# A recorded schedule gets a model of the DMA queue; transposes move between TensorE and DMA; outputs get a second PSUM bank

## The chip, the core and the metric

The kernel runs on one core of one Trainium2 chip. The metric is the device time of one execution in microseconds (us), as the median of several. PE is TensorE, PEld its weight loads, DVE is VectorE, ACT ScalarE, POOL GpSimd, SP SyncE, which issues all DMAs here. A transfer lands when its data can be used. PSUM is the memory that PE writes its results to; it is divided into banks.

## The reference, cut to what matters

```python
# q, k, v, f_logit: (4, 8, 768, 48) float32
f = 1.0 / (1.0 + np.exp(-f_logit))
for t in range(S):
    state = f[:, :, t, :, None] * state + np.einsum('bhd,bhe->bhde', k[:, :, t], v[:, :, t])
    y[:, :, t] = np.einsum('bhd,bhde->bhe', q[:, :, t], state)
x = y.transpose(0, 2, 1, 3).reshape(3072, 384)
out = np.maximum(x @ w_in, 0.0) ** 2 @ w_out      # w_in 384 x 2048, w_out 2048 x 384
```

It is a gated linear attention with a state per head, and a feed-forward with squared relu on its result.

## The kernel before

It works in 24 chunks of 128 tokens, six for each of four sequences. A chunk passes through a line of short steps on all engines: logarithms and sums of the gates (a1, p1), their exponentials (a2), scaled q and k (v1q, v1k, in the tile az), their transposes (p2 and v2 on PE and DVE or ACT, or t2 by DMA), scores (p3, v3), the result yp (p4), its bf16 copy ys (a3), the transpose of that (p6, v6, to xT), and the state sz for the next chunk (p5, s1, s2). The feed-forward's first layer (hp, L439) takes chunks 6 and later in threes, 384 columns wide; the second (op, L484) gives 128 tokens at a time.

No order is written down. Each step is given to a planner with its engines, durations, predecessors and buffers. The planner plays the program through, always starting the best ready step, and then records the instructions in that order. Each engine runs its own list in order. A planner that is wrong about time therefore makes engines stand behind an instruction whose data are late, while others could run.

```python
        plan.add(f"{n}{i}", "SP", 1.03, fn, take=["io_" + n], rank=0, land=1.9)      # a load: 1.03 us on SP, lands 1.9 us later
...
        plan.add(f"w{kind}{s}", "SP", 2.3, fn, take=["wst"], rank=0, land=1.9)       # a fourth of w_in or w_out
...
        xbar = i >= XBAR                                                             # XBAR = 8
        if xbar:
            plan.add(f"v2.{i}", "SP", 1.5, t2, after=[f"v1k.{i}", f"v1q.{i}"], take=["ts"], rank=-2, land=3.5)
        else:
            both(f"v2.{i}", 0.65, 1.0, v2, after=[f"p2.{i}"], take=["ts"], give=[f"tr:p2.{i}"])
...
        plan.add(f"s2.{i}", "POOL", 1.0, s2, after=[f"s1.{i}"] + ([f"p4.{i - 1}"] if c else []), give=[f"en:a2n.{i}"])
...
            tag = "h" if g == NG - 1 and tt else "o"                                 # the bank of an output; "o" is one bank
```

Loads go first in, first out: three chunks, w_in, three chunks, w_out, the rest. Dummy matmuls (idle, L513) fill PE's gaps until 40 us.

## Time and profile before

| | before |
|---|---|
| median time | 199.9 us (198.7 to 200.1) |
| span of the profile | 197.0 us |
| PE, DVE, ACT, POOL busy | 90%, 68%, 67%, 20% |
| bytes moved by DMA, share of the queue's time | 34.1 MB, 87.9% |
| DMA transposes | 16, of q and k of chunks 8 to 23 |

The prediction shows the lines that matter. One more view belongs here, the timeline of POOL in the kernel before, as it dates the arrival of the chunks. Columns: start, length, engine, line, operation, operands, and in brackets the idle time ahead with its releaser.

```profile
58.95 0.51 POOL L284 CAST vz<-io_v 128x384 bf16<-128x384 f32 x1 [0.76 <-DMA io_v<-in_v_dram]
...
62.81 0.51 POOL L284 CAST vz<-io_v 128x384 bf16<-128x384 f32 x1 [0.59 <-DMA io_v<-in_v_dram]
```

These are the casts of v for chunks 7 and 8; both start when the load lands.

### The profile page before, as it was taken

How to read it: one execution, taken by the hardware profiler on the slowest of the kernel's cores; microseconds unless marked ns; L12 is line 12 of the kernel's file. 1: busy time of each engine (PE TensorE's matmuls, PEld its weight loads, DVE VectorE, ACT ScalarE, POOL GpSimd, SP SyncE). 2: the span in 40 equal slices, each digit the busy share in tenths (PEclk: the TensorE clock that was granted, in tenths of full speed). 3: DMA queues.
4: the chain of work that ended last, by engine and by line, in shares of the span. 5: the costliest groups of instructions: out<-in, count | busy, mean ns of one | idle time of the engine just before them, and what ended most of it. 6: DMA issues, size and time to landing. Idle time of an engine off the chain costs nothing.

```text
span 197.0 us, 4806 instructions
## 1 busy us (share of the span) xinstructions
PE 178.3 (90%) x1837; PEld 120.4 (61%) x1837; DVE 134.0 (68%) x285; ACT 132.8 (67%) x281; POOL 38.5 (20%) x80
## 2 busy tenths in 40 slices
PE   5986888769899889998899999799999999999993
PEld 5865777668676556555566666466665666665661
DVE  4578878877779638887897897687889743343300
ACT  4362777757885436888898798686866958655410
POOL 5153001610133304202312320132331300000000
PEclk9999999999999999999999999999999999999999
DMA  7999999899889999999899999998999531111012
GB/s 129 188 163 295 367 167 203 196 379 240 172 164 227 171 223 215 206 193 190 169 200 212 208 207 163 213 195 183 203 215 190 113 95 40 42 39 37 31 58 80
DMA packets 123927, 34.39 MB, mean 175 GB/s; under 512 B 117248, under 2 KB 122368, under 8 KB 123904
## 3 DMA queue, kind: packets, MB, share of 16 engines
q1 hardware_dynamic: 123904, 34.09, 87.9%
q8 instruction: 14, 0.23, 0.5%
q14 instruction: 9, 0.07, 0.1%
HBM read 25.17 MB, written 4.72 MB: 152 GB/s over the span
## 4 chain that ended last, share of the span: by engine, by line
PE 47%; SPq 22%; DMA 20%; ACT 3%; DVE 2%; issue 2%; POOL 2%; POOLq 0%; ACTq 0%
PE op L484 22%; SPq L206 19%; PE hp L439 17%; DMA io_v<-in_v_dram 16%; DMA io_f<-in_f_logit_dram 4%; SPq L222 2%; PE yp L369 2%; PE at L346 2%; POOL vz L284 2%; PE ds L400 1%; DVE am L353 1%; PE xp L383 1%; PE pc L290 1%; SPq L333 1%; ACT ob L494 1%
## 5 line engine op out<-in xcount | busy, mean ns | idle before, releaser
L439 PE MATMUL hp<-xT,w_in 128*128 128x384 bf16 (+2 forms) x528 | 79.1, 282 | 3.7 <-ACT hr L446 2.4
L484 PE MATMUL op<-w_out,hT 128*128 128x384 bf16 x384 | 77.0, 326 | 1.6 <-ACT w_out L237 0.9
L439 PEld LDWEIGHTS <-w_in 128*128 128x128 bf16 x528 | 41.9, 97 | 20.2 <-issue 2.8
L446 ACT ACTIVATE hr<-hp 128x384 bf16<-128x384 f32 (+1 forms) x85 | 42.8, 509 | 15.1 <-PE hp L439 14.3
L484 PEld LDWEIGHTS <-hT 128*128 128x128 bf16 x384 | 35.4, 98 | 23.2 <-issue 2.1
L455 DVE TENSOR_TENSOR hT<-hr 128x384 bf16<-128x384 bf16 (+1 forms) x80 | 30.7, 390 | 23.0 <-ACT hr L446 22.0
L353 DVE TENSOR_TENSOR am<-at,ut 128x512 bf16<-128x512 f32 x48 | 31.4, 683 | 3.8 <-PE at L346 3.6
L417 POOL TENSOR_TENSOR sz<-tm,en 48x192 bf16<-48x192 f32 x40 | 21.1, 528 | 41.9 <-DVE tm L408 9.5
L284 POOL CAST vz<-io_v 128x384 bf16<-128x384 f32 x24 | 13.9, 581 | 72.8 <-DMA io_v<-in_v_dram 72.7
L453 ACT ACTIVATE hT<-hr 128x384 bf16<-128x384 bf16 (+1 forms) x40 | 21.5, 539 | 4.4 <-DVE hr L448 3.5
L279 ACT ACTIVATE e<-io_f 128x384 f32<-128x384 f32 x24 | 12.5, 521 | 15.0 <-DMA io_f<-in_f_logit_dram 14.8
L448 DVE TENSOR_SCALAR hr<-hp 128x384 bf16<-128x384 f32 (+1 forms) x35 | 20.1, 580 | 2.4 <-PE hp L439 2.1
L310 DVE TENSOR_TENSOR az<-io_k,ep 128x384 bf16<-128x384 f32 x24 | 14.0, 583 | 6.8 <-ACT ep L300 5.8
L314 DVE TENSOR_TENSOR az<-io_q,en 128x384 bf16<-128x384 f32 x24 | 13.8, 573 | 4.2 <-DMA io_q<-in_q_dram 4.2
L300 ACT ACTIVATE ep<-pc 128x384 f32<-128x384 f32 x24 | 11.8, 490 | 4.6 <-PE pc L293 4.5
L513 PE MATMUL idle<-zero 128*128 128x128 bf16 x141 | 13.4, 250 | 1.0 <-DVE zero L249 1.0
L494 ACT COPY ob<-op 128x384 f32<-128x384 f32 x18 | 8.5, 473 | 8.5 <-PE op L484 8.4
L280 ACT ACTIVATE pz<-e 128x384 bf16<-128x384 f32 x24 | 12.5, 523 | 0.8
L306 ACT ACTIVATE en<-pc 128x388 f32<-128x388 f32 (+1 forms) x24 | 11.9, 496 | 0.0
L513 PEld LDWEIGHTS <-zero 128*128 128x128 bf16 x141 | 10.6, 114 | 1.2 <-DVE zero L249 1.0
L290 PE MATMUL pc<-pz,ut 128*128 128x384 bf16 x24 | 8.0, 332 | 3.4 <-ACT pz L280 3.2
L377 ACT CAST ys<-yp 128x384 bf16<-128x384 f32 x15 | 7.2, 477 | 5.3 <-PE yp L369 5.1
(43 smaller groups left out, 146.4 us busy)
## 6 DMA issues: line engine op xcount, KB each, us to landing
io_f<-in_f_logit_dram SPq DMA_DIRECT2D x24, 192.0 KB, 4.2
io_k<-in_k_dram SPq DMA_DIRECT2D x24, 192.0 KB, 4.4
io_q<-in_q_dram SPq DMA_DIRECT2D x24, 192.0 KB, 4.4
io_v<-in_v_dram SPq DMA_DIRECT2D x24, 192.0 KB, 4.0
out_dram<-ob SPq DMA_DIRECT2D x24, 192.0 KB, 2.2
wi_f<-in_moe_w_in_dram SPq DMA_DIRECT2D x4, 768.0 KB, 7.4
wo_f<-in_moe_w_out_dram SPq DMA_DIRECT2D x4, 768.0 KB, 8.0
ts<-az SPq DMA_TRANSPOSE x16, 3.6
```

What stands on the lines that cost most here:

```text
L206: nc.sync.dma_start(t, srcs[n][b].rearrange("h s d -> s h d")[c * C:(c + 1) * C])
L284: nc.gpsimd.tensor_copy(vz[i % 3], st["v", i])
L310: nc.vector.tensor_mul(az[i % 3][:, H:, :D], st["k", i], st["ep", i])
L353: nc.vector.tensor_mul(t, st["at", i][x], ut4)
L417: nc.gpsimd.tensor_mul(nx[r, :, D * x:D * (x + 1)], st["tm", i][r, :, D * x:D * (x + 1)], st["en", i][r, HD:HD + NP].unsqueeze(2).to_broad ...
L439: nc.tensor.matmul(hp[:, x, :], w_in[:, ks, (f + x) * C:(f + x + 1) * C], xT[:, ks, lo:lo + W], start=(ks == 0), stop=(ks == KS - 1), skip ...
L446: nc.scalar.activation(hr[:, :m, :], st["hp", c0, f][:, :m, :], AFT.Relu)
L448: nc.vector.tensor_scalar_max(hr[:, :m, :], st["hp", c0, f][:, :m, :], 0.0)
L453: nc.scalar.activation(st["hT", g][:, f:f + m, lo:lo + W], hr[:, :m, :], AFT.Square)
L455: nc.vector.tensor_mul(st["hT", g][:, f:f + m, lo:lo + W], hr[:, :m, :], hr[:, :m, :])
L484: nc.tensor.matmul(st["o", i], hT[:, fs, tt * C:(tt + 1) * C], w_out[:, fs, :], start=(fs == 0), stop=(fs == FS - 1))
L513: nc.tensor.matmul(idle, zero, zero)
```

## The change

The intent is a planner with a model of how transfers queue. In this model SP is busy for a short time for each DMA, the transfers run one after the other, a ring of limited size makes SP wait, and data land 1.2 us after their last byte. Durations are fitted anew. With that model, the DMA transposes of q and k start at chunk 14 in place of 8; from chunk 18 the result is transposed by DMA too; four buffers in place of three for az, vz and en and three in place of two for ys; outputs of chunks 19 and 21 take the transposes' PSUM bank (23 already has another).

```diff
+    FIRST, RECEIPT = 0.4, 1.2
+    RING = 3000
...
+                    if s.data:
+                        us, size = s.data
+                        while sum(z for e, z in queue if e > end) + size > self.RING:
+                            end = min(e for e, z in queue if e > end)
+                        moved_to = max(moved_to, end + self.FIRST) + us
+                        queue.append((moved_to, size))
...
-                    fin = end + s.land
+                    fin = moved_to + self.RECEIPT if s.data else end + s.land
...
-    XBAR = 8
+    XBAR = 14
+    XBAR2 = 18
...
-                pz=2, az=3, vz=3, ts=3, am=2, ys=2, ep=2, en=3)
+                pz=2, az=4, vz=4, ts=3, am=2, ys=3, ep=2, en=4)
...
-            plan.add(f"{n}{i}", "SP", 1.03, fn, take=["io_" + n], rank=0, land=1.9)
+            plan.add(f"{n}{i}", "SP", 0.45, fn, take=["io_" + n], rank=0, data=(1.07, 1024))
...
-        plan.add(f"p1.{i}", "PE", 0.27, p1, after=[f"a1.{i}"] + ([f"p4.{i - 2}"] if i > 1 else []), ...
+        plan.add(f"p1.{i}", "PE", 0.26, p1, after=[f"a1.{i}"] + ([f"p4.{i - 3}"] if i > 2 else []), ...
...
-            plan.add(f"v2.{i}", "SP", 1.5, t2, after=[f"v1k.{i}", f"v1q.{i}"], take=["ts"], rank=-2, land=3.5)
+            plan.add(f"v2.{i}", "SP", 1.25, t2, after=[f"v1k.{i}", f"v1q.{i}"], take=["ts"], rank=-2, data=(1.7, 1024))
...
+        if xbar2:
+            plan.add(f"v6.{i}", "SP", 0.7, t6, after=[f"a3.{i}"] + ([f"v6.{i - 1}"] if o else []),
+                     take=["xT"] if o == 0 else [], give=[f"ys:a3.{i}"], rank=-2, data=(0.9, 384))
...
-            tag = "h" if g == NG - 1 and tt else "o"
+            tag = "h" if g == NG - 1 and tt else "tr" if i > max(XBAR, XBAR2) and i % 2 else "o"
```

Cut are the new durations of some twenty steps, most of them a few per cent shorter, and the fourth buffers' index arithmetic. The diff moves code, so line numbers shift: L439 (first layer) is now L459, L484 (second layer) L504, L237 (cast of weights on ACT) L248, L284 (cast of v) L295.

## The prediction

> **What bounds the kernel now.** I read the page first, its busy line and the slices.
>
> ```profile
> PE 178.3 (90%) x1837; PEld 120.4 (61%) x1837; DVE 134.0 (68%) x285; ACT 132.8 (67%) x281; POOL 38.5 (20%) x80
> ...
> PE   5986888769899889998899999799999999999993
> ...
> DMA  7999999899889999999899999998999531111012
> ```
>
> Two limits stand in a row. The DMA row is full until slice 31 (about 155 us) and then empty, while PE is at eight or nine tenths from slice 10 nearly to the end. Whether DMA or PE sets the end is told by the busy times in stretches of 15 us.
>
> ```profile
> 30.00:45.00 15.00, 11.59 (x189) 9.78 (x188) 12.28 (x25) 9.92 (x21) 4.32 (x8) 1.00 1.02 265
> 45.00:60.00 15.00, 13.63 (x185) 10.53 (x185) 11.27 (x26) 11.46 (x26) 2.65 (x4) 1.00 0.87 185
> ...
> 105.00:120.00 15.00, 15.00 (x143) 9.28 (x141) 12.71 (x27) 12.69 (x29) 3.53 (x7) 1.00 1.25 207
> ...
> 165.00:180.00 15.00, 15.00 (x97) 9.10 (x95) 5.38 (x15) 9.20 (x20) 0.00 (x0) 1.00 0.11 41
> ```
>
> Columns after the length: PE, PEld, DVE, ACT and POOL busy, then clock and DMA share. From 105 us PE has no slack, and it still works for 38 us after the last load has landed. So the end is PE work plus the idle time that PE collected before. Where that lies is told by the timeline of PE (in brackets the idle time ahead, and its releaser); I show its gaps between 39 and 76 us that matter, and the ends of that stretch.
>
> ```profile
> 39.03 1.50 PE L439 MATMUL hp<-xT,w_in 128*128 128x128 bf16 x24 [0.35 <-ACT xT L390]
> ...
> 42.87 0.83 PE L439 MATMUL hp<-xT,w_in 128*128 128x128 bf16 x12 [1.52 <-ACT hr L446]
> ...
> 50.24 0.81 PE L484 MATMUL op<-w_out,hT 128*128 128x384 bf16 x4 [0.94 <-ACT w_out L237]
> ...
> 65.80 0.33 PE L383 MATMUL xp<-ident,ys 128*128 128x128 bf16 x3
> ...
> 68.89 0.33 PE L400 MATMUL ds<-vz,az 128*128 128x96 bf16 x4 [0.88 <-POOL vz L284]
> ...
> 72.83 0.65 PE L484 MATMUL op<-w_out,hT 128*128 128x384 bf16 x3 [0.57 <-ACT ob L494]
> ...
> 74.92 0.33 PE L383 MATMUL xp<-ident,ys 128*128 128x128 bf16 x3
> ...
> 76.01 0.65 PE L439 MATMUL hp<-xT,w_in 128*128 128x384 bf16 x3
> ```
>
> With one of 0.33 us at 59.51 the gaps from 39.03 to 76.01 make 4.2 us. After 76 us the same view has five, 2.9 us in all, of which 1.95 wait for the cast of v on POOL (0.60, 1.00, 0.35). The 1.52 us goes back to ACT, which stands in line behind a cast whose weights have not landed:
>
> ```profile
> 41.81 0.51 ACT L237 CAST w_out<-wo_f 128x384 bf16<-128x384 f32 x1 [2.83 <-DMA wo_f<-in_moe_w_out_dram]
> ```
>
> The last two lines of PE above are the other half. At 76.01 the first 384-wide matmul of the feed-forward starts, the one for chunks 6 to 8 together. It waits for chunk 8. POOL casts v of chunk 7 at 58.95 us and PE transposes its result at 65.80, 6.9 us later. v of chunk 8, the first whose q and k go through the DMA transpose, is cast at 62.81, and its result is transposed at 74.92, 12.1 us later. By then 92 of the 96 output matmuls that chunks 0 to 5 give are done: PE is living on its last work.
>
> **What the Trainium skill says.** "TensorE: Matmul & The Clock Gate", section "Wait — 56ns, not 53.3ns?": start to start is N ÷ 2.4 GHz plus about 2.5 ns; 162.5 ns for 384 columns. The trace agrees: the chain has 12 output matmuls in 1.95 us. I use this form as unit price. The same page, "Architectural detail: the array is 16× 32×32, not 1× 128×128", says that ACT and DVE are strictly first in, first out; the 2.83 us above is such a case. "DMA: Bandwidth & Descriptors", section "Latency and other measured facts": about 600 ns to the first byte; the new model takes 0.4 us, and 1.2 us for the receipt. No trace splits it so, but the sum fits: the model (12 loads of 1.07, four weights of 2.75, 12 loads, one weight, plus 0.4 and 1.2, plus 0.45 for the first issue and 0.74 before it) puts the first w_out slice at 42.2 us, and the trace has its casts at 41.81. The old model (1.03, 2.3, 1.9) gives 38.9 with the same start, 2.9 us too early: just the length of that wait. "PSUM — Partial Sum Buffer", "Summary: rules for kernel authors": read one bank while matmuls write another; the 0.57 us on ob is the wait that a second output bank removes.
>
> **The change part by part.** (a) The model. It moves instructions and removes none. The order of PE's instructions, before and after, is known from the built programs; with unit prices I sum the real work (fillers left out) ahead of a landmark. Landmark one is the first matmul of chunk 3's feed-forward: 16.3 us of work in both. Landmark two is the first output matmul that needs the last w_out slice: 24.6 us before, 28.1 us after. That is the gain of the better model: 3.5 us of work that stood behind a wait now stands ahead of it. In the old kernel landmark two is at 50.24 us, and the loads ahead of it are unchanged, so it cannot come earlier.
>
> (b) Transposes of q and k for chunks 8 to 13 go back to PE: 6 × 8 = 48 matmuls at 55.5 ns, +2.7 us of PE, and six copies of about 0.6 us on DVE. Transposes of the result from chunk 18 leave PE: 6 × 3 at 55.5 ns, -1.0 us, and six copies of 0.3 us. Net on PE +1.7 us (159.0 to 160.6), all on the path. DMA loses six transposes; a chunk comes every 6.2 us with them (v of chunk 10 cast at 75.59, of chunk 23 at 155.91) and every 5.0 without (chunks 6 to 9), so about 7 us of DMA, which is beside PE's work and worth nothing by itself. Its real worth is that chunk 8 takes about 7 us instead of 12, so its columns are ready near 62.8 + 6.9 + 0.4 = 70.1 us.
>
> (c) Fourth buffers and the second output bank: at most the 0.57 us and part of the 2.9.
>
> The sum. Between 39.03 and 76.01 PE did 30.6 us of work by unit prices (16.3 to 46.9) in 37.0 - 4.2 = 32.7 us without gaps: factor 1.07. After the change: chunk 3 ready at about 38.0, as its transposes no longer stand behind the sums of chunk 4 (an estimate of mine); landmark two at 38.0 + 1.07 × 11.8 = 50.6, which just meets the weights; from there to the first 384-wide matmul 47.1 - 28.1 = 19.0, times 1.07 = 20.3, with 1.0 us of gaps (1.8 there before): 71.9 us, and chunk 8 is there at 70.1. That is 4.1 us earlier than 76.01. After it the old kernel did 112.1 us of work in 117.8 - 2.9 = 114.9 (factor 1.025); the new one has 160.6 - 47.1 = 113.5, times 1.025 = 116.3, with gaps of 2.0 (no waits for v, but DVE has more to copy at 75 to 90 us, where it was busy 13.37 of 15): PE ends at 190.2 instead of 193.8. The end behind it (copy, store: 3.2 us) stays. Span 193.4 instead of 197.0; time 199.9 - 3.6 = 196.3 us.
>
> **The rivals.** First, the transposes taken off the DMA pull the end in by their 7 us, to about 193, as the DMA row is full. Against: PE is full from 105 us on and has 38 us of work after the last load; loads that end near 148 shorten no PE work. Second, DVE and ACT become the bound: six copies more, at a stage where both have over 12 of 15 us busy; PE then loses 2 to 3 us more around 75 to 100 us, and the time stays at 199. For it: the copies all stand on DVE in the new order. Against: 15 relus move from DVE to ACT, and the sum of both engines changes by some 2 us in 267. Third, a new wait: the last chunk's result goes through the DMA, 3.6 us in the old trace for the larger transposes. Between the last attention matmul and the first use of its result stand 3 first-layer and 22 output matmuls, 25 × 162.5 ns = 4.1 us; if copy, issue and transfer take 6 us together, PE waits 2 us and the time is 198. For the short latency speaks that the DMA is nearly empty by then.
>
> **Range and chances.** The floor is no idle time after landmark two: 50.2 + 20.3 + 116.3 + 3.2 = 190.0 span, 192.9. The ceiling is the added 1.7 us with nothing gained but the chunk 8 wait, about 199. I take 193.3 to 199.0. Two per cent is 195.9, just under my figure: faster 0.43, same 0.52, slower 0.05.
>
> **What would show it.** Right: the first 384-wide matmul at 71 to 73 us; no wait of ACT or DVE over 1 us for the weights after 40 us; the last v cast near 148 us or before; PE busy 15.0 of 15 after 75 us; the last PE instruction near 190. Wrong: that matmul still at 75 or later (model step), new gaps of PE with DVE or ACT as releasers over 4 us in all after 76 us (second rival), a gap ahead of the last chunks' first-layer matmuls (third), or an end that follows the last load (first).

## The result

The changed kernel takes 193.6 us (193.4 to 193.6, four runs); the kernel before 199.3 beside it (198.4 to 200.1). The ratio is 0.971, interval 0.966 to 0.976: faster. A ratio here compares the fast runs of two kernels in the same rounds, so it is not quite the ratio of the medians quoted. Of the kernel before, two runs beside the experiments (200.6 and 200.5 us) were slow and are left out of the ratios. The experiments ran on three chips, where the kernel before took 199.3, 197.9 and 198.7 us, so kernels are compared by their ratios.

The page of the changed kernel answers the first fence of the prediction:

```profile
PE 179.8 (94%) x1874; PEld 122.5 (64%) x1874; DVE 131.6 (69%) x278; ACT 134.6 (70%) x290; POOL 39.2 (20%) x79
...
PE   6987898798999999999999999999999999989993
...
DMA  6998999999799999999879989999888652211112
```

The span fell by 5.1 us while PE's busy time rose by 1.5 us: what went is PE's idle time. The nines of PE begin at slice 11 and break once, at slice 35. The DMA row keeps its shape: the loads end about where they did. The same stretches of 15 us as before:

```profile
30.00:45.00 15.00, 12.98 (x217) 10.87 (x215) 13.78 (x27) 11.21 (x25) 4.45 (x7) 1.00 1.10 260
45.00:60.00 15.00, 14.16 (x173) 10.40 (x170) 10.17 (x22) 10.71 (x24) 2.37 (x4) 1.00 0.98 212
...
105.00:120.00 15.00, 15.00 (x145) 9.42 (x143) 11.09 (x23) 12.43 (x29) 2.95 (x6) 1.00 0.99 193
...
165.00:180.00 15.00, 13.95 (x87) 8.19 (x86) 5.01 (x14) 8.05 (x17) 0.00 (x0) 1.00 0.11 35
```

The early stretches gain PE time (in the first, 3.00 us before and 3.27 after are dummy matmuls); the late one, which had none to lose before, loses 1.05 us. The timeline of PE shows the landmarks, and that gap:

```profile
51.46 0.81 PE L504 MATMUL op<-w_out,hT 128*128 128x384 bf16 x4
...
71.11 0.33 PE L394 MATMUL xp<-ident,ys 128*128 128x128 bf16 x3
...
72.47 1.14 PE L459 MATMUL hp<-xT,w_in 128*128 128x384 bf16 x6
...
168.59 1.15 PE L459 MATMUL hp<-xT,w_in 128*128 128x384 bf16 x6 [1.05 <-DMA xT<-ys]
```

The first 384-wide matmul starts 3.5 us earlier than at 76.01. Chunk 8's result is transposed at 71.11; its v is cast by POOL 6.6 us earlier:

```profile
64.47 0.51 POOL L295 CAST vz<-io_v 128x384 bf16<-128x384 f32 x1
```

The last line of PE is its one listed gap after 72.47: PE waits for the DMA transpose of the last chunk's result. The cast that ACT used to wait 2.83 us for has moved behind other work, and starts at 42.05 with no wait:

```profile
41.58 0.58 ACT L466 ACTIVATE hr<-hp 128x512 bf16<-128x512 f32 x1
42.05 0.50 ACT L248 CAST w_out<-wo_f 128x384 bf16<-128x384 f32 x1
42.46 0.60 ACT L466 ACTIVATE hr<-hp 128x512 bf16<-128x512 f32 x1
```

**One account for all runs.** The prediction prices PE's real work by its unit price and sums it in the built order. With the start of the first 384-wide matmul (call it W) and the end of the last matmul, both read in the timeline of PE, that splits what is not real work into two parts: ahead of W (W minus the work before it; dummy matmuls count as idle) and after W (the end minus W minus the work left). Small gaps that the timeline doesn't list are in it too, and time in which PE counts as busy but takes longer than the price, so it is an estimate of lost time, made in the same way for every kernel. The last lines of PE, before and after, give its end (185.82 + 7.96 = 193.78 and 180.62 + 7.96 = 188.58):

```profile
185.82 7.96 PE L484 MATMUL op<-w_out,hT 128*128 128x384 bf16 x48
...
180.62 7.96 PE L504 MATMUL op<-w_out,hT 128*128 128x384 bf16 x48
```

| kernel | W | work before W | lost before W | work after W | PE ends | lost after W |
|---|---|---|---|---|---|---|
| before | 76.0 | 46.9 | 29.1 | 112.1 | 193.8 | 5.7 |
| changed | 72.5 | 47.3 | 25.2 | 113.3 | 188.6 | 2.8 |

So 3.9 us came from before W and 2.9 us after it, and 1.6 us of work was added: 5.2 us net at the end of PE.

**Is the new model right about time?** The planner in kernel.py is plain Python, so it can be played off the chip and its planned casts of v set beside those of the trace. In the kernel before they come later and later than planned, 1.0 us for chunk 0 and 6.7 for chunk 23; in the changed kernel all 24 lie within 1.6 us of the plan.

### The profile page after: what moved, and what is told of

Its sections match the earlier page's. It is cut to its first block, busy times and chain, and to the rows that moved or that the text cites. A ratio compares the mean times of both kernels' runs of the same rounds, so it can differ in the third digit from the quotient of the medians.

```text
span 191.9 us, 4888 instructions
## 1 busy us (share of the span) xinstructions
PE 179.8 (94%) x1874; PEld 122.5 (64%) x1874; DVE 131.6 (69%) x278; ACT 134.6 (70%) x290; POOL 39.2 (20%) x79
## 4 chain that ended last, share of the span: by engine, by line
PE 75%; ACT 7%; DMA 6%; SPq 6%; DVE 3%; issue 2%; DVEq 0%; ACTq 0%
PE op L504 31%; PE hp L459 30%; SPq L217 6%; PE yp L380 4%; DMA wi_f<-in_moe_w_in_dram 4%; PE at L357 3%; ACT hr L466 3%; DMA xT<-ys 2%; PE pc L301 2%; PE tr L333 2%; PE ds L420 2%; PE xp L394 1%; ACT w_in L248 1%; ACT hT L473 1%; PE pc L304 1%
## 5 line engine op out<-in xcount | busy, mean ns | idle before, releaser
L459 PE MATMUL hp<-xT,w_in 128*128 128x384 bf16 (+2 forms) x528 | 78.7, 282 | 3.2 <-DMA xT<-ys 1.1
L504 PE MATMUL op<-w_out,hT 128*128 128x384 bf16 x384 | 76.3, 326 | 0.4 <-ACT ob L514 0.4
L466 ACT ACTIVATE hr<-hp 128x384 bf16<-128x384 f32 (+1 forms) x103 | 51.9, 510 | 17.0 <-PE hp L459 15.5
L459 PEld LDWEIGHTS <-w_in 128*128 128x128 bf16 x528 | 41.3, 97 | 21.2 <-issue 1.6
L475 DVE TENSOR_TENSOR hT<-hr 128x384 bf16<-128x384 bf16 (+1 forms) x84 | 32.0, 386 | 30.4 <-ACT hr L466 28.7
L504 PEld LDWEIGHTS <-hT 128*128 128x128 bf16 x384 | 35.5, 97 | 22.3 <-issue 0.5
L437 POOL TENSOR_TENSOR sz<-tm,en 48x192 bf16<-48x192 f32 x40 | 22.2, 555 | 64.1 <-DVE tm L428 26.1
L295 POOL CAST vz<-io_v 128x384 bf16<-128x384 f32 x24 | 14.2, 591 | 51.7 <-DMA io_v<-in_v_dram 51.1
L473 ACT ACTIVATE hT<-hr 128x384 bf16<-128x384 bf16 (+1 forms) x36 | 19.4, 546 | 1.5 <-DVE hr L468 0.8
L514 ACT COPY ob<-op 128x384 f32<-128x384 f32 x21 | 10.0, 474 | 13.8 <-PE op L504 13.7
L325 DVE TENSOR_TENSOR az<-io_q,en 128x384 bf16<-128x384 f32 x24 | 16.1, 673 | 0.0
L341 DVE COPY ts<-tr 128x1024 bf16<-128x1024 bf16 x14 | 9.6, 685 | 5.7 <-PE tr L333 5.7
L388 ACT CAST ys<-yp 128x384 bf16<-128x384 f32 x18 | 8.6, 477 | 5.1 <-PE yp L380 5.1
L468 DVE TENSOR_SCALAR hr<-hp 128x384 bf16<-128x384 f32 (+1 forms) x17 | 9.9, 585 | 2.4 <-PE hp L459 2.0
```

Source lines behind the costliest of these rows:

```text
L295: nc.gpsimd.tensor_copy(vz[i % 4], st["v", i])
L325: nc.vector.tensor_mul(az[i % 4][:, :H, :D], st["q", i], st["en", i][:, :HD].rearrange("p (h d) -> p h d", d=D))
L437: nc.gpsimd.tensor_mul(nx[r, :, D * x:D * (x + 1)], st["tm", i][r, :, D * x:D * (x + 1)], st["en", i][r, HD:HD + NP].unsqueeze(2).to_broad ...
L459: nc.tensor.matmul(hp[:, x, :], w_in[:, ks, (f + x) * C:(f + x + 1) * C], xT[:, ks, lo:lo + W], start=(ks == 0), stop=(ks == KS - 1), skip ...
L466: nc.scalar.activation(hr[:, :m, :], st["hp", c0, f][:, :m, :], AFT.Relu)
L473: nc.scalar.activation(st["hT", g][:, f:f + m, lo:lo + W], hr[:, :m, :], AFT.Square)
```

## The experiments

Theory 1 is the prediction's: the better model fills PE ahead of the weights and removes stalls (most of the gain), chunk 8's shorter way is the condition for it, and room on the DMA is worth nothing by itself. The rival: moving the transposes of q and k off the DMA is what pays.

### The two parts alone, and each undone

b_newmodel keeps the new planner and durations, and undoes the rest:

```diff
-    XBAR = 14
-    XBAR2 = 18
+    XBAR = 8
+    XBAR2 = 24
-                pz=2, az=4, vz=4, ts=3, am=2, ys=3, ep=2, en=4)
+                pz=2, az=3, vz=3, ts=3, am=2, ys=2, ep=2, en=3)
```

(and p1 after p4 of two chunks before, and outputs in one bank)

> The new planner model and durations alone: transposes of q and k by DMA from chunk 8 as in the kernel before, no DMA transpose of the result, old buffer counts, one output bank. Theory 1 (the better model fills PE ahead of the last w_out slice and removes stalls behind late data; this is most of the gain): the built order has 28.1 us of work ahead of landmark two, as after; landmark two near 51.5 us; chunk 8 still takes 12 us from its v cast, so the first 384-wide matmul starts at 75 to 76 us and PE idles 2 to 3 us for it; then 111.8 us of work at factor 1.02: time 194 to 196, at least half of the gain. Rival (moving the transposes off the DMA is what pays): 197.5 or more.

Measured: 197.6 us, ratio 0.995 (0.990 to 1.001).

b_xbar14 is the kernel before with one number changed:

```diff
-    XBAR = 8
+    XBAR = 14
```

> The kernel before with one number changed: DMA transposes of q and k from chunk 14 in place of 8, old model. Theory 1: the order still has only 24.6 us of work ahead of landmark two, PE has 2.6 us more work, so the time is 199 to 201, no gain, though the first 384-wide matmul comes early (near 73 us, with 44.7 us of work before it). Rival (DMA relief and a faster chunk 8 are what pay): 194 to 196.

Measured: 196.5 us, ratio 0.990 (0.984 to 0.997).

a_oldmodel is the changed kernel with the old planner's transfers and durations; for the transposes of the result, which that planner never had, I took a landing of 3.0 us, a guess:

```diff
-            plan.add(f"{n}{i}", "SP", 0.45, fn, take=["io_" + n], rank=0, data=(1.07, 1024))
+            plan.add(f"{n}{i}", "SP", 1.03, fn, take=["io_" + n], rank=0, land=1.9)
```

(and so on for all transfers and durations)

> The changed kernel with the old model put back (issue and landing times and durations of the old planner; everything else as changed: chunk 14, chunk 18, fourth buffers, second output bank). Theory 1: work ahead of landmark two falls from 28.1 to 24.8 us, waits for w_out on ACT and DVE come back; time 196.5 to 198.5. Rival: stays within 1 us of the changed kernel, 193 to 194.5.

Measured: 196.8 us, ratio 0.992 (0.986 to 0.999). ACT and DVE wait for w_out again, 2.3 us each in all (4.5 and 3.1 in the kernel before, none listed in the changed kernel).

a_xbar8 undoes the other part in the changed kernel:

```diff
-    XBAR = 14
+    XBAR = 8
```

> The changed kernel with DMA transposes of q and k from chunk 8 again. PE has 2.6 us less work (158.0 against 160.6), but chunk 8 is late again and DMA is fuller. Theory 1 with the prediction's chunk 8 step: first 384-wide matmul at 75 to 76 us with 47.2 us of work before it, all 96 output matmuls used up, PE idle 2 to 3 us there; these cancel the 2.6 us, time 193 to 194.5. Rival (DMA relief pays): 196 or more, loads end near 155 us and PE waits for v on POOL after 76 us by 2 us or more.

Measured: 198.2 us, ratio 0.998 (0.992 to 1.004); its profiled run, at 200.3 us, had a mean clock of 0.991, so I read no small difference from its trace.

Neither theory as it stood survives. The model alone gives a sixth of the gain and not half; chunk 14 alone gives more, against theory 1, but only a third, against the rival. Each of the two undone takes most of the gain away. So 2.6 us of PE work less in a_xbar8 bought nothing.

All four of these kernels gave wrong numbers, relative error 0.0497 to all digits. The reason is told below; it touches one step of POOL, and I use their times with that reservation.

### The fourth corner, and the small parts

after_ctl is the changed kernel unedited.

> The changed kernel, unedited, as the measure for the runs of this call (the first call had none, and its runs were on another chip than the result may have been). Both theories: 193 to 194.5, ratio 0.97 within 0.007. It also tells whether the remark 'relative error 0.0497' of the first four runs is the edits' or this kernel's own; I expect its own, as it was the same to all digits four times.

Measured: correct, 194.0 us (192.1 to 195.0), ratio 0.976 (0.968 to 0.985).

b_new14 is b_newmodel with chunk 14:

```diff
-    XBAR = 8
+    XBAR = 14
```

> New model and durations plus chunk 14 for q and k, but no DMA transpose of the result, old buffers, one output bank: the fourth corner of a square with the kernel before, new model alone (ratio 0.995) and chunk 14 alone (0.990). If the two parts add up, 0.985 (196.4 us). Theory 2, formed after the first call (the parts need each other: the order that the new model makes is only as good as chunk 8's way over PE lets it be): 0.978 or less, 195 us or less, first 384-wide matmul near 72.5 us. Theory 1 as predicted (model most of it) has fallen.

Measured: correct, 194.5 us, ratio 0.980 (0.973 to 0.987). The sum of the parts, 0.985, lies inside the interval, so this square alone doesn't show that they need each other. With the small parts in, undoing the model costs 2.1% (0.971 to 0.992), where the model alone gave 0.5%; that points to it.

a_noyx takes the DMA transposes of the result and the second bank out of the changed kernel:

```diff
-    XBAR2 = 18
+    XBAR2 = 24
-            tag = "h" if g == NG - 1 and tt else "tr" if i > max(XBAR, XBAR2) and i % 2 else "o"
+            tag = "h" if g == NG - 1 and tt else "o"
```

> The changed kernel without DMA transposes of the result and with one output bank, buffers as changed. PE has 1.0 us more work, but the 1.05 us wait for the last chunk's transpose before the last group goes, so the time should be as the changed kernel within 0.5 us. If the second bank or the emptier PE were worth more (rival), it is 1.5 us slower or more.

Measured: correct, 194.8 us, ratio 0.983 (0.975 to 0.992); its PE ends at 188.3 us, beside 188.9 in after_ctl.

The corner without the small parts has PE end at 188.7 us, as in the changed kernel (188.6 and 188.9). So buffers, second bank and transposes of the result have no effect in the traces that I could see. By the clock a_noyx is 0.8 us slower in the median and b_new14 0.6 us, which is within the spread of the runs. Against the ratio of the first result, 0.971, up to about 1% for the small parts is not excluded. (One run of the kernel before on this chip, 200.4 us, had a mean clock of 0.982; without it the four ratios of this section and the next experiment would be about 0.002 higher.) It fits that the 1.0 us that the transposes take off PE comes back as the 1.05 us wait for the last of them.

a_oldqueue keeps the new durations, but books transfers the old way:

```diff
-                    if s.data:
+                    if False:
-                    fin = moved_to + self.RECEIPT if s.data else end + s.land
+                    fin = end + s.land
```

(with the old issue and landing times, and the guess of 3.0 us)

> The changed kernel with the new durations but the old account of transfers (issue 1.03 and 2.3 us, landing 1.9 us, no queue). Between the old model (0.992) and the changed kernel. If the queue of transfers is what the model brings: 196.5 us as with the old model altogether. If the durations are: 194 us. Work ahead of landmark two is 26.8 us, between 24.8 and 28.1.

Measured: correct, 197.0 us, ratio 0.992 (0.985 to 0.999), as with the whole old model. So it is the queue that the changed kernel needs from the new model, not the durations. The surprise is where: W is at 71.0 us with 46.8 us of work before it, lost time 24.2, no worse than the changed kernel's 25.2; after W it loses 6.3 us. The timeline of PE there, of this run:

```profile
136.50 0.33 PE L420 MATMUL ds<-vz,az 128*128 128x96 bf16 x4 [0.54 <-POOL vz L295]
...
144.07 0.27 PE L380 MATMUL yp<-vz,am 128*128 128x48 bf16 x4 [0.37 <-DVE am L364]
145.38 0.33 PE L420 MATMUL ds<-vz,az 128*128 128x96 bf16 x4 [0.54 <-POOL vz L295]
```

PE again stands behind a cast of v whose load comes later than the plan had it: by 1.0 us for chunk 0 and 9.8 for chunk 23. After W such listed waits make 1.62 us here and 1.95 in the kernel before, and there are none in any kernel whose queue is modelled. But there are none after W in chunk 14 alone and in a_oldmodel either, which book the old way, so the wait for v is one form of the loss and not the whole of it.

### Is it chunk 8, or the other five?

a_chunk9 lets chunk 8 go over PE and sends chunks 9 to 13 by DMA:

```diff
-    XBAR = 14
+    XBAR = 9
```

> The changed kernel with DMA transposes of q and k from chunk 9: chunk 8 goes over PE, chunks 9 to 13 over the DMA. It parts two readings of why chunk 14 pays. Reading A, as predicted (only chunk 8's way counts, DMA relief is worth nothing): the first 384-wide matmul comes at about 70.5 us (45.3 us of work before it, plus 25.2), then 113.1 us of work with 2.8 idle: PE ends at 186.4, time 191.4, faster than the changed kernel. Reading B (the six transposes taken off the DMA count in the stretch after it, as the idle time there was 5.7 to 8.4 us in all kernels with DMA transposes from chunk 8 and 1.8 to 2.9 with the new model from chunk 14): the same start, but 6 us idle or more after it: time 194.5 or more.

Measured: 196.2 us, ratio 0.988 (0.984 to 0.992), wrong numbers (relative error 0.0431). W came at 70.66 us, as reading A has it. But PE ended at 191.2 us:

```profile
70.66 1.14 PE L459 MATMUL hp<-xT,w_in 128*128 128x384 bf16 x6
...
185.19 6.01 PE L504 MATMUL op<-w_out,hT 128*128 128x384 bf16 x36
```

So 7.4 us are lost after W. Reading B holds: the five other transposes do cost. Other pairs agree, though chunk 8 moves in them too: the lost time after W falls from 5.7 to 2.5 us from the kernel before to chunk 14 alone, and from 6.5 to 1.9 from the model alone to both. Each edit is planned anew, so what is measured is the transposes together with the order that they lead to; no run holds the order still. Busy time in six stretches of 16 us from 72 to 168 us, the sum line (length, then PE, PEld, DVE, ACT, POOL, then means); first the kernel before:

```profile
sum 96.00, PE 92.37 PEld 57.26 DVE 74.62 ACT 75.70 POOL 20.42; mean PE 15.40 PEld 9.54 DVE 12.44 ACT 12.62 POOL 3.40
```

a_chunk9:

```profile
sum 96.00, PE 92.77 PEld 56.33 DVE 72.26 ACT 72.72 POOL 20.13; mean PE 15.46 PEld 9.39 DVE 12.04 ACT 12.12 POOL 3.35
```

the changed kernel:

```profile
sum 96.00, PE 95.41 PEld 60.28 DVE 71.94 ACT 77.67 POOL 20.70; mean PE 15.90 PEld 10.05 DVE 11.99 ACT 12.94 POOL 3.45
```

With the transposes on the DMA, PE is idle 3.2 to 3.6 us of the 96; with them on PE 0.6. DVE and ACT together are hardly fuller where PE idles (150.3 and 145.0 us, against 149.6), so they do not look like what it lacks. In a_chunk9 the idle time is spread. This is what one sees of it in its timeline of PE:

```profile
86.71 1.62 PE L504 MATMUL op<-w_out,hT 128*128 128x384 bf16 x9 [0.57 <-ACT ob L514]
...
149.04 0.65 PE L504 MATMUL op<-w_out,hT 128*128 128x384 bf16 x3 [0.57 <-ACT ob L514]
153.27 0.65 PE L504 MATMUL op<-w_out,hT 128*128 128x384 bf16 x3 [0.66 <-ACT ob L514]
```

PE has only outputs of one chunk after the other at hand, and waits for each bank to be emptied. It is short of fresh chunks: v of chunk 13 is cast at 94.0 us there and at 94.6 in the kernel before, but at 89.5 in the changed kernel, and the last v at 164.3 there, at 155.2 in the changed kernel. Whether the transposes delay chunks by the room they take on the DMA or by their own way of 3.5 us in each chunk's line is not separated by these runs; both go away together.

### The two single parts again

> The new model alone once more, the same kernel, as its first run gave wrong numbers in a call where all four kernels did, and had no unedited changed kernel beside it. Correct this time, 0.995 within 0.007 of before; first 384-wide matmul near 74.6 us.

Measured: wrong again with the same error, 197.5 us, ratio 0.997 (0.992 to 1.002), W at 73.9 us.

> Chunk 14 alone in the kernel before, once more, for the same reason. Correct this time, 0.990 within 0.007 of before; first 384-wide matmul near 71.3 us.

Measured: wrong again, 196.3 us, ratio 0.988 (0.984 to 0.993), W at 72.1 us.

The times repeat; the expectation that the numbers would be right fell. Waits for late data end chunk 8's line in b_newmodel_r (timeline of PE), as the prediction expected for such a kernel:

```profile
68.79 0.65 PE L504 MATMUL op<-w_out,hT 128*128 128x384 bf16 x3 [0.57 <-ACT ob L514]
...
73.11 0.34 PE L394 MATMUL xp<-ident,ys 128*128 128x128 bf16 x3 [0.57 <-DVE ys L388]
...
73.89 1.14 PE L459 MATMUL hp<-xT,w_in 128*128 128x384 bf16 x6 [0.21 <-DVE xT L399]
```

**The wrong numbers.** Seven runs of five kernels were wrong, always by the same amount for the same edits, on two chips, and so not by chance. The cause is read in the code and played off the chip; no run was left to try the mended kernels. The state has two buffers, sz. s2 of chunk i writes the one that p4 of chunk i - 1 reads, and the planner is told so only inside a sequence (`if c`, in the line for s2 shown above). At the first chunk of a sequence the edge is missing. Where a plan lets s2 of chunk 12 or 18 run ahead of p4 of chunk 11 or 17, that chunk reads the next sequence's state. Playing the programs' arithmetic through in their recorded order, off the chip, puts s2 ahead in exactly the five wrong kernels; the output with that state in place has errors of 0.0493 and 0.0426, close to the 0.0497 and 0.0431 measured, all of them in the rows of chunk 17 (chunk 11 in a_chunk9). Both kernels of this study have the same hole; their orders happen to avoid it. The wrong kernels run the same instructions. With the edge put in, the planner gives every engine the same list as before (in a_oldmodel two steps of POOL change places); what changes is who waits for whom at that one step. Of the listed gaps of PE only one waits for sz, 0.30 us in a_chunk9, so the hole says little against their times.

### A version that goes on from here

a_last_pe leaves the last chunk's result to PE:

```diff
-        xbar, xbar2 = i >= XBAR, i >= XBAR2
+        xbar, xbar2 = i >= XBAR, XBAR2 <= i < NCH - 1
```

> The changed kernel, but the result of the very last chunk (23) is transposed on PE and not by DMA; chunks 18 to 22 stay on the DMA. The one gap of PE after 76 us in the changed kernel, 1.05 us for that transpose, goes; PE has 0.17 us more work. If it is as it looks, 0.8 us faster than the changed kernel: 192.8 us, ratio 0.967 to 0.972. If the gap only moves to the next wait (rival), equal to it.

Measured over five rounds: correct, 192.4 us (191.8 to 192.9), ratio 0.970 (0.966 to 0.973). The gap is gone. The timeline of PE at the same place:

```profile
163.41 0.33 PE L394 MATMUL xp<-ident,ys 128*128 128x128 bf16 x3
163.58 1.14 PE L504 MATMUL op<-w_out,hT 128*128 128x384 bf16 x6
164.56 1.14 PE L459 MATMUL hp<-xT,w_in 128*128 128x384 bf16 x6
```

Six output matmuls now cover the way from the transpose to the last group, where 22 did not cover the DMA. It is the fastest version in the median; against the changed kernel, which was not run beside it, the intervals overlap, so by the clock "about 1 us faster" is likely and not shown. That the wait went is shown.

### The experiments in one table

a_xbar8 is left out for its clock.

| kernel | ratio | W | work before W | lost before W | work after W | PE ends | lost after W |
|---|---|---|---|---|---|---|---|
| changed, old model | 0.992 | 70.6 | 44.7 | 25.9 | 115.9 | 191.4 | 4.9 |
| changed, results over PE, one output bank (a_noyx) | 0.983 | 72.2 | 47.3 | 24.9 | 114.3 | 188.3 | 1.8 |
| model alone (2nd run) | 0.997 | 73.9 | 47.2 | 26.7 | 111.8 | 192.2 | 6.5 |
| chunk 14 alone (2nd run) | 0.988 | 72.1 | 44.7 | 27.4 | 116.9 | 191.5 | 2.6 |
| both (b_new14) | 0.980 | 72.5 | 47.3 | 25.2 | 114.3 | 188.7 | 1.9 |
| changed, chunk 9 | 0.988 | 70.7 | 45.3 | 25.4 | 113.1 | 191.2 | 7.4 |
| changed, old booking of transfers | 0.992 | 71.0 | 46.8 | 24.2 | 113.8 | 191.2 | 6.3 |
| changed, last chunk on PE | 0.970 | 71.6 | 47.3 | 24.3 | 113.5 | 186.7 | 1.6 |

One caution on the early column. The two runs of chunk 14 alone have the same order, and their W differs by 0.7 us (71.3 and 72.1), as their loads do (v of chunk 8 is cast at 61.70 and 62.56); less than 1 us in that column is not a difference. Where the old booking loses its time differs too: ahead of W in chunk 14 alone (27.4, and 2.6 after it), after W in a_oldqueue (24.2 and 6.3); no run shows why.

## Why the prediction was right or wrong

**The figure was right**: 193.6 us in the range of 193.3 to 199.0, 2.7 us under the 196.3 predicted, and near the lower edge. The outcome that I gave 0.43, faster by over 2%, is the one that came; the favoured one, within 2%, did not. That the time lies in the range is partly luck: the sum lacked a gain that the first rival named, and that rival's figure, about 193, was nearer.

**What bounds the kernel: right.** In both kernels the end is PE's work plus the idle time that it collects: the span fell by 5.1 us while PE's busy time rose by 1.5.

**Waits behind late weights: right, but mis-sized.** The waits of ACT and DVE for w_out are gone. "That is the gain of the better model: 3.5 us of work that stood behind a wait now stands ahead of it" took landmark two as fixed at 50.24 us. It moved to 51.46, since the work that now stands ahead of it is not all ready in time. What counts is the lost time there: 50.2 - 24.6 = 25.6 us before and 51.5 - 28.1 = 23.4 after, so 2.2 us in place of 3.5. The model alone gave 0.3 and 0.5% in its two runs.

**W at 71.9 us: nearly right**, 72.47: landmark two came 0.9 us late, at 51.46 for 50.6, and the stretch from there took 21.0 us for 21.3. Chunk 8's line was right: from cast to transpose of its result 6.6 us (64.47 to 71.11), where 6.9 was taken.

**"The transposes taken off the DMA ... worth nothing by itself": wrong.** This is the step that failed. I set its worth by chunk 8 alone, as PE listed only 2.9 us of gaps after W and worked for 38 us after the last load. a_chunk9 keeps chunk 8 on PE and loses 7.4 us after W, where the changed kernel loses 2.8. The first rival was right that those transposes pay, and wrong that the end follows the loads. Without them the last v is cast at 143.6 us in chunk 14 alone, 12.3 earlier than in the kernel before, and PE ends 3.1 earlier; in the changed kernel, where the transposes of the result go over the DMA, it is cast at 155.2, so my sign "near 148 us or before" failed, and the time fell all the same. What does move is the middle: v of chunk 13 comes 5.1 us earlier than before. PE then has chunks at hand, and that is worth more than the 2.2 us of PE work for five chunks. My list of gaps could not show it. Of the 7.4 us in a_chunk9 PE is idle for 3.5, of which 3.0 are listed; in the other 3.9 it counts as busy, but takes longer than the price. In the changed kernel these are 1.2 and 1.6 us. I had carried the second part over from the kernel before as a fixed factor, 1.025 or 2.8 us. It isn't fixed; what makes it up is not shown, but for the end of each broken stream: a 384-wide matmul counts 0.32 us where it stands alone and 0.16 within a stream.

**Part (c) and the second rival.** "At most the 0.57 us and part of the 2.9": no effect seen. The 0.57 us could not go by it: that wait, at 72.83 us, is one of the outputs of chunks 0 to 5, and only outputs 19 and 21 get the second bank. DVE did fill up (14.69 of 15 us at 75 to 90 us, where I feared for 13.37), and PE still was busy 14.88 of 15; that rival fell.

**The third rival: right in kind.** I gave 4.1 us of matmuls as cover for the last chunk's DMA transpose and said that PE waits if it takes longer. From 163.31, where the matmuls behind the last attention matmul start, to the first use at 168.59 it took 5.3 us, and PE waited 1.05. I left it out of the central sum, so that sum should have been 1 us higher there; the gain after W covered it.

**The sum.** Predicted: 4.1 us before W, PE's end at 190.2. Measured: 3.5 us earlier at W, end 188.6. The 1.6 us between them and 1.1 us in the step from span to time, where I took off the difference of the spans from a median 1.1 us above the profiled run, make the 2.7 us. After W the sum had 2.8 us above the price and 2.0 of gaps; measured are 1.6 and 1.2. Two small slips: the work before W is 47.3 us and not 47.1, and 18 relus moved from DVE to ACT and not 15 (ACT has 85 before, 103 after).

## What to carry to other kernels

When an order comes from a model, the booking of shared transfers in it can matter more than a few per cent on each duration; set the planned times beside the traced ones, as a lag that grows shows the error. Its worth can depend on the rest: here two parts at about 0.4% and 1.1% alone made 2.0% together, which hints at it and doesn't prove it. Judge an engine's lost time by span minus priced work and not by the list of its visible gaps, as time in which it counts as busy above the price can outweigh those that are listed. And a planner's edges are part of correctness: an order that happens to be right hides a missing one, until some number is tuned.

## What the Trainium skill lacked or had wrong

- "DMA: Bandwidth & Descriptors" gives constraints and an effective bandwidth for DMA transposes, and "VectorE: DVE Perf Modes" one time for a 128x128 block, but neither has issue time and time to landing for one of this size within SBUF. In the changed kernel 128 x 1024 bf16 took 1.32 us of SP in the median and landed 3.5 us after issue; 128 x 384 took 1.20 us and 3.2 us (2.4 in a_chunk9): in the same kernel three eighths of the bytes are hardly cheaper.
- "VectorE: DVE Perf Modes" prefers TensorE for a 128x128 transpose where PSUM can take it, but no page tells what a DMA transpose costs an engine that is short of chunks. Here five chunks' transposes on the DMA took 2.2 us of work off PE and cost it 4.6 us of lost time (7.4 against 2.8; an estimate from priced work).
